# Subtracting the low parts of the feed-forward input on VectorE instead of GpSimd

## The chip, the cores and the metric

One core of a Trainium2 chip. The time is device microseconds of one launch, the median of three runs; the profile is that of one execution. The engines are TensorE (PE, with its weight loads as PEld), VectorE (DVE), ScalarE (ACT), GpSimd (POOL) and SyncE (SP), which issues the transfers.

## The reference

Block-causal attention over 64 heads (8 batches of 8 heads, 576 positions, 64 channels), then a low-rank mixing over positions and a feed-forward block with a residual.

```python
scores = scale * np.matmul(q, k.transpose(0, 1, 3, 2))
scores = np.where(mask, scores, -1000000000.0)
scores = scores - np.max(scores, axis=-1, keepdims=True)
attn = np.exp(scores)
attn = attn / (np.sum(attn, axis=-1, keepdims=True) + 1e-09)
attn_out = np.matmul(attn, v)
...
h = xt @ U @ V
u = x + h.transpose(0, 2, 1)
ch = np.maximum(u @ w_ch1, 0.0) @ w_ch2
return (u + ch).astype(np.float32)
```

## The kernel before, in words

Products are made more exact by splitting an operand into a high part (a cast to fp32r) and a low part (the operand less its high part), and adding three products: high by high, high by low, low by high.

Attention goes head by head: scores (L962 for the first 12 heads, L966 and L967 after them), row maxima on VectorE (L980, tile mx), exponentials on ScalarE (L991, p), reciprocal row sums on VectorE (L1007, L1008, rv), the rows multiplied by them on GpSimd (L1017, p), transposes on TensorE (L1050), from head 10 on a high and a low part of the transposed rows (ph on ScalarE L1027, pl on VectorE L1069), and the products with v (L1109, before that L1093). After every second head the mixing of two heads (`mix`) ends in the products of L1163; its small operand t3 has its low rows written by VectorE in L1154 (32x128, two inputs in SBUF). L1168 adds its result to attention's: that is u, 128 of the 512 channels.

The hidden layer has 2048 columns. Its first half is done by `ffn_chunk`, for 16 chunks of 288 positions. A chunk has four blocks k of 128 channels. For each, ScalarE casts u to the high part uh (L445) and GpSimd subtracts it to get the low part ul (L447). Eight column blocks f follow, each of 12 products (L465: w1h by uh, w1l by uh, w1h by ul), a ReLU on ScalarE (hh, L470) and its low part on VectorE (hl, L473); then the second layer's products (L488) and the sum with the input on VectorE (L494, ot). The first two chunks are done in two passes of four blocks f, so that there are 18 sets of four subtractions, 72 in all. The tiles uh and ul exist once, so a set waits until TensorE has read the last one's. The second half of the hidden layer (`block_products`, L659) follows when attention and the first half are done; its weights are loaded and combined by VectorE (L331 to L345, L548, L551) once attention has ended.

The order on all engines is set by the class `Plan`: each step is added with an engine, a cost in ns, a priority and its buffers, and `issue` plays the steps out in an event simulation, giving each free engine the ready step of the lowest priority value. Attention has priorities from 10 to 64000, the chunks' products 1e6 and more (they fill what attention leaves of TensorE), the chunks' other steps, the subtraction among them, -1. A step with `port=True`, and every step of GpSimd, is only given out while no other such step is running in the simulation. The instructions stand in the order so found, and each engine takes its own in that order.

```python
for x in later:
    heapq.heappush(q, x)
...
port = port or tasks[n][7]
end = now + tasks[n][1]
```

Of the kernel before, what the change touches and what calls it, by code (L numbers as in the profile page):

```python
# [26 lines left out]
T = 288  # L27
# [110 lines left out]
class Plan:  # L138
# [8 lines left out]
    def add(self, engine, ns, prio, fn, reads=(), writes=(), hold=(), after=0, port=False):  # L147

        n = len(self.tasks)
        deps = set()  # L150
        for b in reads:
            deps.update(b.writers)
            b.readers.append(n)
        for b in hold:
            deps.update(b.readers, b.writers)
        for b in writes:
            deps.update(b.readers, b.writers)
            b.writers, b.readers = [n], []
        deps.discard(n)
        slots = {b for b in (*reads, *writes) if b.pool is not None}  # L160
        for b in slots:
            b.users += 1
        self.tasks.append((engine, ns, prio, fn, deps, after, slots, port or engine == "POOL"))
# [76 lines left out]
def _act(n, sbuf=False):  # L240
    return (93 if sbuf else 52) + 0.833 * n


def _dve(n):
    return 69 + 1.042 * n


def _pe(*ns, m=()):

    m = [*m, *[P] * len(ns)][1 : len(ns)] + [P]  # L250
    return sum(max(0.85 * w, n * COL) for n, w in zip(ns, m))
# [3 lines left out]
def attention_then_mixer(  # L255
# [10 lines left out]
    nc = tc.nc  # L266
# [10 lines left out]
    def f32(ap):  # L277
        return ap.bitcast(F32)
# [29 lines left out]
    def take(r, name):  # L308
        n = used[name] = used.get(name, -1) + 1
        return r[n % len(r)]  # L310
# [120 lines left out]
    def ffn_chunk(c, w, wb, fr=range(FC), turn=0):  # L431

        b, o = c // CPB, (c % CPB) * T
        banks, done = banks_f if c < NCHUNK - 1 else Part(banks_f, banks_f), ffn_done[c]
        E, F = -1.0, 1e6 + (1300 + 300 * c if turn else 1000 * c)
        ur = ur_r[c % 2]
        for k in range(KC):
            if b > 0 or turn:
                add(
                    "SP", 630, E, lambda k=k: nc.sync.dma_start(out=ur[k].ap, in_=u_d[b][:, k, o : o + T]),  # L440
                    u_s[b][k].parts, [ur[k]], after=DL,
                )
        for k in range(KC):
            uh, ul = uh_r[k], ul_r[k]
            add("ACT", _act(T, True), E, lambda u=ur[k], h=uh: nc.scalar.copy(h.ap, u.ap), [ur[k]], [uh])  # L445
            add(
                "POOL", 780, E, lambda u=ur[k], h=uh, l=ul: nc.gpsimd.tensor_sub(l.ap, u.ap, f32(h.ap)),  # L447
                [ur[k], uh], [ul],
            )
            if turn:  # L450
                add(
                    "SP", 630, E, lambda k=k: nc.sync.dma_start(out=ur[k].ap, in_=o_d[b][:, k, o : o + T]),
                    [o_s[c][k]], [ur[k]], after=DL,
                )
        hs = {}
        for f in fr:
            ps = Buf(pool=banks)
            fs = slice(f * P, (f + 1) * P)
            ops = [(wn, k, m) for wn, m in (("w1h", uh_r), ("w1l", uh_r), ("w1h", ul_r)) for k in range(KC)]
            for g in range(0, len(ops), GM):  # L460

                def products(g=g, ps=ps, fs=fs, ops=ops):
                    for i in range(g, g + GM):
                        wn, k, m = ops[i]
                        nc.tensor.matmul(ps[:, :T], w()[wn][:, k, fs], m[k].ap, start=(i == 0), stop=(i == len(ops) - 1))  # L465

                sub = ops[g : g + GM]
                add("PE", _pe(*[T] * GM), F, products, [m[k] for _, k, m in sub] + [wb["w1"][f * P // CW][k] for _, k, _ in sub], [ps])
            th, tl = take(hh_r, "hh"), take(hl_r, "hl")
            add("ACT", _act(T), E, lambda ps=ps, th=th: nc.scalar.activation(th.ap, ps[:, :T], AF.Relu), [ps], [th])  # L470
            add(
                "DVE", _dve(T), E,
                lambda ps=ps, th=th, tl=tl: nc.vector.scalar_tensor_tensor(  # L473
                    out=tl.ap, in0=ps[:, :T], scalar=0.0, in1=f32(th.ap), op0=ALU.max, op1=ALU.subtract
                ),
                [ps, th], [tl],
            )
            hs[f] = (th, tl)
        for m in range(KC):
            ps = Buf(pool=banks)  # L480
            ms = slice(m * P, (m + 1) * P)
            ops = [(wn, f, x) for f in fr for wn, x in (("w2h", 0), ("w2l", 0), ("w2h", 1))]
            for g in range(0, len(ops), GM):

                def products(g=g, ps=ps, ms=ms, ops=ops):
                    for i in range(g, g + GM):
                        wn, f, x = ops[i]
                        nc.tensor.matmul(ps[:, :T], w()[wn][:, f, ms], hs[f][x].ap, start=(i == 0), stop=(i == len(ops) - 1))  # L488

                sub = ops[g : g + GM]  # L490
                add("PE", _pe(*[T] * GM), F, products, [hs[f][x] for _, f, x in sub] + [wb["w2"][f] for _, f, _ in sub], [ps])
            ot = take(ot_r, "ot")
            add(
                "DVE", _dve(T), E, lambda ps=ps, ot=ot, m=m: nc.vector.tensor_add(ot.ap, ps[:, :T], ur[m].ap),  # L494
                [ps, ur[m]], [ot],
            )
            done.writers.append(len(plan.tasks) - 1)
            add(
                "SP", 630, E, lambda ot=ot, m=m: nc.sync.dma_start(out=o_d[b][:, m, o : o + T], in_=ot.ap), [ot],
                [o_s[c][m]], after=DL,  # L500
            )
# [723 lines left out]
    for n in range(2):  # L1225
        for c in range(CPB):
            ffn_chunk(c, lambda: wa, wab, range(n * FH, (n + 1) * FH), n)
    for c in range(CPB, NCHUNK):
        ffn_chunk(c, lambda: wa, wab)
# [40 lines left out]
```

## Time and profile before

| | |
|---|---|
| median of 3 runs | 1183.15 us (1181.67 to 1183.31) |
| the profiled execution | 1182.37 us |
| its span, first to last instruction | 1180.6 us |
| busy: TensorE, weight loads | 1164.1 us (99%), 1131.4 us (96%) |
| busy: VectorE, ScalarE, GpSimd | 936.2 us (79%), 774.9 us (66%), 451.2 us (38%) |
| instructions of GpSimd, of VectorE | 582, 2009 |

Shares over the whole span are averages over three stages: attention with the first half as fill (to about 657 us), the rest of the first half (to about 820 us), and the second half. GpSimd works in the first two alone. Products of TensorE overlap, so that a product of 288 columns is shown with 0.29 us where one starts every 0.13 us.

### The profile page before, as it was taken

The page shows a single profiled execution, that of the slowest core. Times are in us where ns is not written, and L with a number is a line of the kernel's source. Part 1 is how long each engine was busy: PE and PEld are TensorE (multiplying, and loading weights), DVE is VectorE, ACT ScalarE, POOL GpSimd, SP SyncE. Part 2 cuts the span into 40 slices and gives each one's busy share as a digit, 9 for nine tenths or more (in the row PEclk, how much of TensorE's full clock was granted, in tenths as well). Part 3 has the DMA queues.
Part 4 walks back from the last instruction along what each step waited for, and adds up shares of the span by engine and source line. Part 5 has one row for each costly group of instructions (what it writes and reads, how often), then busy time and mean ns, then how long its engine had stood idle before and what let it go on. Part 6 is the DMA issues. An engine that isn't in the chain of part 4 may idle for free.

```text
span 1180.6 us, 25204 instructions
## 1 busy us (share of the span) xinstructions
PE 1164.1 (99%) x8988; PEld 1131.4 (96%) x8988; DVE 936.2 (79%) x2009; ACT 774.9 (66%) x1924; POOL 451.2 (38%) x582
## 2 busy tenths in 40 slices
PE   9989999999999999999999999999999999999998
PEld 7778999999999999999999999999999999999998
DVE  6898887877887877777877587327989889889887
ACT  7888888989888888898887342114544444444443
POOL 5556876676757666766674122110000000000000
PEclk9999999999999999999999999999999999999999
DMA  4445565433433433443331434211132132132121
GB/s 142 141 153 154 160 177 140 116 115 108 114 112 110 123 105 111 114 117 110 112 94 52 142 113 145 66 52 50 61 122 71 51 121 70 53 121 62 60 81 41
DMA packets 75884, 122.69 MB, mean 104 GB/s; under 512 B 8944, under 2 KB 52976, under 8 KB 75760
## 3 DMA queue, kind: packets, MB, share of 16 engines
q1 hardware_dynamic: 75760, 121.09, 34.8%
q8 instruction: 71, 1.16, 0.4%
q14 instruction: 53, 0.43, 0.1%
HBM read 76.23 MB, written 29.49 MB: 90 GB/s over the span
## 4 chain that ended last, share of the span: by engine, by line
PE 81%; DVE 8%; ACT 7%; issue 2%; DMA 1%; SPq 0%; POOL 0%; ACTq 0%; DVEq 0%; POOLq 0%
PE bb L659 30%; PE bf L465 11%; PE bf L488 10%; PE ba L1050 7%; PE ba L1109 6%; PE bg L488 4%; PE bg L465 4%; ACT p L991 3%; DVE mx L980 2%; PE ba L967 2%; PE ba L966 2%; PE ba L1134 1%; PE bw L966 1%; PE ba L1148 1%; DVE pl L1069 1%
## 5 line engine op out<-in xcount | busy, mean ns | idle before, releaser
L1017 POOL TENSOR_SCALAR p<-p,rv 128x192 f32<-128x192 f32 (+4 forms) x320 | 171.8, 551 | 156.8 <-DVE rv L1008 85.2
L659 PE MATMUL bb<-hh,w1l 128*128 128x288 f32 x704 | 170.1, 295 | 0.0
L659 PE MATMUL bb<-hh,w1h 128*128 128x288 f32 x704 | 169.4, 295 | 0.0
L1069 DVE TENSOR_TENSOR pl<-ba,ph 128x512 fp32r<-128x512 f32 x216 | 113.7, 550 | 17.9 <-ACT ph L1027 15.7
L991 ACT ACTIVATE p<-ba,mx 128x448 f32<-128x448 f32 (+2 forms) x248 | 114.8, 466 | 16.4 <-DVE mx L980 12.8
L1050 PE MATMUL ba<-ident,p 128*128 128x128 f32 x768 | 122.8, 275 | 2.7 <-POOL p L1017 1.5
L659 PE MATMUL bb<-hl,w1h 128*128 128x288 f32 x576 | 123.0, 295 | 0.1
L659 PEld LDWEIGHTS bb<-hh,w1l 128*128 128x128 f32 x704 | 122.9, 190 | 0.0
L659 PEld LDWEIGHTS bb<-hh,w1h 128*128 128x128 f32 x704 | 121.9, 188 | 0.0
L488 PE MATMUL bf<-hh,w2h 128*128 128x288 f32 x384 | 118.8, 309 | 0.9 <-DVE hl L473 0.9
L488 PE MATMUL bf<-hl,w2h 128*128 128x288 f32 x384 | 113.5, 295 | 0.0
L488 PE MATMUL bf<-hh,w2l 128*128 128x288 f32 x384 | 112.7, 294 | 0.0
L447 POOL TENSOR_TENSOR ul<-ur,uh 128x288 fp32r<-128x288 f32 x72 | 61.5, 880 | 127.2 <-PE bf L465 80.9
L613 ACT CAST hh<-hb 128x576 fp32r<-128x576 f32 x98 | 65.9, 672 | 60.6 <-PE bb L659 59.3
L1027 ACT CAST ph<-ba 128x512 fp32r<-128x512 f32 x216 | 98.8, 491 | 9.1 <-PE ba L1050 7.8
L980 DVE TENSOR_REDUCE mx<-ba 128x1 f32<-128x448 f32 (+3 forms) x248 | 95.1, 406 | 10.1 <-PE ba L967 7.5
L1050 PEld LDWEIGHTS ba<-ident,p 128*128 128x128 f32 x768 | 89.9, 141 | 8.3 <-POOL p L1017 3.4
L659 PEld LDWEIGHTS bb<-hl,w1h 128*128 128x128 f32 x576 | 91.9, 188 | 0.4 <-DVE hl L614 0.4
L1109 PE MATMUL ba<-ph,vs 128*128 128x256 f32 (+3 forms) x432 | 89.9, 262 | 0.0
L465 PE MATMUL bf<-uh,w1l 128*128 128x288 f32 x392 | 82.1, 305 | 0.0
L913 POOL TENSOR_TENSOR k<-raw,k 64x576 fp32r<-64x576 f32 x52 | 75.1, 1444 | 2.1 <-POOL p L1017 0.5
L912 POOL TENSOR_TENSOR q<-raw,q 64x576 fp32r<-64x576 f32 x52 | 74.0, 1422 | 4.5 <-issue 2.1
(173 smaller groups left out, 3357.7 us busy)
## 6 DMA issues: line engine op xcount, KB each, us to landing
raw<-in_qk_dram SPq DMA_DIRECT2D x63, 288.0 KB, 3.9
st<-in_w_dram SPq DMA_DIRECT2D x32, 512.0 KB, 3.7
o_d<-ot SPq DMA_DIRECT2D x72, 144.0 KB, 1.8
vr<-in_v_dram SPq DMA_DIRECT2D x32, 320.0 KB, 3.7
ur<-u_d SPq DMA_DIRECT2D x64, 144.0 KB, 2.4
whole<-o_d SPq DMA_DIRECT2D x32, 288.0 KB, 3.1
out_dram<-whole SPq DMA_DIRECT2D x31, 288.0 KB, 2.2
ur<-u_d SPq DMA_DIRECT2D x30, 288.0 KB, 3.3
```

Of the source, the lines that this page charges most:

```text
L465: nc.tensor.matmul(ps[:, :T], w()[wn][:, k, fs], m[k].ap, start=(i == 0), stop=(i == len(ops) - 1))
L488: nc.tensor.matmul(ps[:, :T], w()[wn][:, f, ms], hs[f][x].ap, start=(i == 0), stop=(i == len(ops) - 1))
L659: nc.tensor.matmul(bank[:, i, :T], x()[:, w(k)], p.ap[:, k, :], start=first and n == 0, stop=last and n == len(ops) - 1)
L912: add("POOL", 1380, pr, lambda: nc.gpsimd.tensor_sub(q1[top], raw[top, 0:S], f32(q2[top])), [raw, q2], [q1])
L913: add("POOL", 1380, pr, lambda: nc.gpsimd.tensor_sub(k2[top], raw[top, S : 2 * S], f32(k1[top])), [raw, k1], [k2])
L980: lambda i=i, at=at: nc.vector.tensor_reduce(out=mx[: P if i else 64, i : i + 1], in_=view(i, at), op=ALU.max, axis=AX.XY if wide else AX. ...
L991: nc.scalar.activation(out.rearrange("p (j k) -> p j k", j=2) if wide else out, view(i, at), AF.Exp, bias=mx[:rows, i : i + 1], accum_out= ...
L1017: lambda x=x, rows=rows, i=i: nc.gpsimd.tensor_scalar(out=x, in0=x, scalar1=rv[:rows, i : i + 1], scalar2=1.0, op0=ALU.mult, op1=ALU.mult),
L1027: add("ACT", _act(n), pr, lambda: nc.scalar.copy(out(), inp()), reads, writes)
L1050: nc.tensor.transpose(out=bank[:, a : a + P], in_=pt_r[i][h % PB[i]][:, j * P : (j + 1) * P], identity=perm.ap)
L1069: "DVE", _dve(m), pr, lambda: nc.vector.tensor_sub(pl[:, low], bank[:, :m], f32(ph[:, low])), [bank, bh], [bl]
L1109: nc.tensor.matmul(bank[0 : c.stop, a:n], vs[:, j, c], x[:, _at(g, j)], start=(i == 0), stop=(i == len(ops) - 1))
```

## The change

The 72 subtractions go from GpSimd to VectorE. Their cost for the planner goes from 780 ns to its formula for VectorE (369 ns at 288 columns), and they are marked as users of the shared port.

```diff
             add("ACT", _act(T, True), E, lambda u=ur[k], h=uh: nc.scalar.copy(h.ap, u.ap), [ur[k]], [uh])
             add(
-                "POOL", 780, E, lambda u=ur[k], h=uh, l=ul: nc.gpsimd.tensor_sub(l.ap, u.ap, f32(h.ap)),
-                [ur[k], uh], [ul],
+                "DVE", _dve(T), E, lambda u=ur[k], h=uh, l=ul: nc.vector.tensor_sub(l.ap, u.ap, f32(h.ap)),
+                [ur[k], uh], [ul], port=True,
             )
```

Because a cost and an engine are changed, the planner finds another order for all engines. Counted over the whole program, GpSimd has 508 instructions for 580 and VectorE 2081 for 2009; TensorE, ScalarE and SyncE have the same number as before in another order.

The first subtraction, on VectorE early in the program (ul, ur and uh as above, z and st the weights in work, mx row maxima, rv reciprocal row sums):

```order
 L980 TENSOR_REDUCE mx_164<-ba_97 128x1
 L980 TENSOR_REDUCE mx_164<-ba_97 64x1
+L447 TENSOR_TENSOR ul_110<-ur_104,uh_106 128x288
 L331 TENSOR_SCALAR z_103<-z_103 128x512
 L332 TENSOR_SCALAR z_103<-z_103 128x512
```

It now stands between a row maximum and a step of the weights. On GpSimd, at the same place of the program (w1l is a low part of weights, p attention's rows), the order of before has:

```order
L1017 TENSOR_SCALAR p_0_148<-p_0_148,rv_166 128x448
L361 TENSOR_TENSOR w1l_213<-z_102,w1h_212 128x512
L447 TENSOR_TENSOR ul_110<-ur_104,uh_106 128x288
L1017 TENSOR_SCALAR p_1_151<-p_1_151,rv_167 128x576
L1017 TENSOR_SCALAR p_0_147<-p_0_147,rv_166 128x320
```

There the rows of p behind it now follow directly on w1l. Later in attention the subtractions come in sets of four. One of them on VectorE in the order of the change (xl and xh are the mixing's operands):

```order
L980 TENSOR_REDUCE mx_165<-bw 128x1
L1139 TENSOR_TENSOR xl_177<-ba_96,xh_176 128x512
L447 TENSOR_TENSOR ul_110<-ur_105,uh_106 128x288
L473 SCALAR_TENSOR_TENSOR hl<-bf_91,hh 128x288
L447 TENSOR_TENSOR ul_111<-ur_105,uh_107 128x288
L447 TENSOR_TENSOR ul_112<-ur_105,uh_108 128x288
L447 TENSOR_TENSOR ul_113<-ur_105,uh_109 128x288
L1139 TENSOR_TENSOR xh_176<-ba_98,xh_176 64x128
```

The set stands around hl of the chunk ahead, which waits for the same products. Over the whole program 52 of VectorE's 72 subtractions stand ahead of its last attention operation (L1168) and 20 behind it; of GpSimd's, 48 stood ahead of its last row of p. On TensorE the last product of attention (L1163) now stands among the first products of a later chunk. Before it stood among the second layer's products:

```order
L488 MATMUL bf_90<-hh,w2l_215 128x288
L488 MATMUL bf_90<-hl,w2h_214 128x288
L1163 MATMUL ba_96<-v_183,t_0_178 128x288
L1163 MATMUL ba_95<-v_183,t_0_178 128x288
L488 MATMUL bf_91<-hh,w2h_214 128x288
```

and now:

```order
L465 MATMUL bf_91<-ul_112,w1h_212 128x288
L465 MATMUL bf_91<-ul_113,w1h_212 128x288
L1163 MATMUL ba_95<-v_183,t_0_178 128x288
L1163 MATMUL ba_96<-v_183,t_0_178 128x288
L465 MATMUL bf_90<-uh_106,w1h_212 128x288
```

Behind that place there were 1224 of the 3072 products of L465 and L488, and now there are 1128, so 96 more of them are ahead of it.

## Rows read from the trace of the kernel before

**Rows 1.** Busy time (share of the span) and instructions, from the profile's page.
```profile
PE 1164.1 (99%) x8988; PEld 1131.4 (96%) x8988; DVE 936.2 (79%) x2009; ACT 774.9 (66%) x1924; POOL 451.2 (38%) x582
```
**Rows 2.** Table by stage: stretch, its length, busy us and instructions, clock, DMA.
```profile
0.00:100.00 100.00, 91.13 (x529) 74.23 (x529) 82.74 (x214) 80.91 (x225) 57.09 (x85) 1.00 0.46 142
100.00:200.00 100.00, 97.94 (x783) 93.98 (x783) 86.34 (x213) 85.82 (x237) 74.77 (x90) 1.00 0.58 165
200.00:650.00 450.00, 447.77 (x3710) 436.43 (x3709) 353.48 (x955) 389.99 (x1101) 296.63 (x385) 1.00 0.38 107
650.00:810.00 160.00, 160.00 (x1212) 159.98 (x1211) 81.94 (x151) 47.81 (x103) 22.74 (x24) 1.00 0.31 97
810.00:1181.00 371.00, 367.25 (x2765) 366.77 (x2763) 331.67 (x479) 170.32 (x261) 0.00 (x0) 1.00 0.25 76
```
**Rows 3.** Waits of TensorE, 0 to 200 us: total us, times, longest.
```profile
PE ba L1050 <- POOL p L1017: 1.5, 2, 0.8
...
PE bf L488 <- DVE hl L473: 0.9, 1, 0.9
```
**Rows 4.** Waits of TensorE, 200 to 650 us: those for VectorE.
```profile
PE ba L1050 <- DVE xh L1139: 0.2, 1, 0.2
PE ba L1163 <- DVE ut L1168: 0.2, 1, 0.2
```
**Rows 5.** Costliest groups of the page: busy us, mean ns | idle before.
```profile
L447 POOL TENSOR_TENSOR ul<-ur,uh 128x288 fp32r<-128x288 f32 x72 | 61.5, 880 | 127.2 <-PE bf L465 80.9 <-PE bg L465 43.5 <-ACT uh L445 2.0
```
**Rows 6.** Waits of TensorE's weight loads over the whole span.
```profile
PEld ba L1050 <- POOL p L1017: 4.6, 11, 0.9
```
**Rows 7.** Lines L614 and L548 by source: shortest/median/longest ns, first and last start.
```profile
L614 DVE TENSOR_TENSOR hl<-ur,hh x46: 746/749/759, 819.3 to 1140.0; 128x576 fp32r<-128x576 f32 x46
...
L548 DVE TENSOR_TENSOR w1l<-whole,w1h x7: 1212/1217/1469, 664.3 to 706.9; 128x1024 fp32r<-128x1024 f32 x7
```
**Rows 8.** Groups of VectorE by line and form: busy us, mean ns | idle before.
```profile
L1168 DVE TENSOR_TENSOR ut<-ba,xt 128x288 f32<-128x288 f32 x56 | 23.9, 446 | 1.3 <-PE ba L1163 1.0
...
L1154 DVE TENSOR_TENSOR t<-tz,t 32x128 fp32r<-32x128 f32 x32 | 13.5, 422 | 2.6 <-ACT t L1153 1.8
```
**Rows 9.** Timeline of VectorE, 640 to 644 us: start us, length us.
```profile
642.44 0.81 DVE L1168 TENSOR_TENSOR ut<-ba,xt 128x288 f32<-128x288 f32 x2
```
**Rows 10.** Line L1154 by source: shortest/median/longest ns, first and last start.
```profile
L1154 DVE TENSOR_TENSOR t<-tz,t x32: 280/284/1526, 36.9 to 655.3; 32x128 fp32r<-32x128 f32 x32
```
**Rows 11.** Timeline of GpSimd, VectorE and TensorE between 322 and 327 us.
```profile
323.78 1.42 POOL L912 TENSOR_TENSOR q<-raw,q 64x576 fp32r<-64x576 f32 x1
...
323.82 1.53 DVE L1154 TENSOR_TENSOR t<-tz,t 32x128 fp32r<-32x128 f32 x1
...
326.62 0.29 PE L488 MATMUL bf<-hl,w2h 128*128 128x288 f32 x1
326.91 0.40 PE L1163 MATMUL ba<-v,t 96*128 96x288 f32 x1
```
**Rows 12.** Timeline of GpSimd, the subtractions: singles, then sets of four.
```profile
43.43 0.98 POOL L447 TENSOR_TENSOR ul<-ur,uh 128x288 fp32r<-128x288 f32 x1
...
113.63 3.37 POOL L447 TENSOR_TENSOR ul<-ur,uh 128x288 fp32r<-128x288 f32 x4
...
192.42 3.09 POOL L447 TENSOR_TENSOR ul<-ur,uh 128x288 fp32r<-128x288 f32 x4
...
541.69 3.12 POOL L447 TENSOR_TENSOR ul<-ur,uh 128x288 fp32r<-128x288 f32 x4 [2.85 <-PE bf L465]
```
**Rows 13.** Timeline of TensorE, 99 to 101 us: the first fill product.
```profile
99.95 0.77 PE L465 MATMUL bf<-uh,w1h 128*128 128x288 f32 x4
```
**Rows 14.** Timeline of VectorE at 706 us and of TensorE at 819 us.
```profile
706.92 1.47 DVE L548 TENSOR_TENSOR w1l<-whole,w1h 128x1024 fp32r<-128x1024 f32 x1
...
819.90 0.30 PE L659 MATMUL bb<-hh,w1h 128*128 128x288 f32 x1
```

## The prediction

> **What bounds the kernel now.** I read the busy shares first, then a table by stage, then who waits for whom in each stage. The profiled execution took 1182.37 us, its span is 1180.6 us, and TensorE is busy for 1164.1 us of that [rows 1], so the 16.5 us of visible idle time are about all that an edit of another engine can give back. The table says where these 16.5 us lie [rows 2]: 8.87 us in the first 100 us, before the feed-forward products can fill the gaps of attention; 2.06 us in the next 100; 2.23 us in the 450 us after that; nothing between 650 and 810 us; the rest is the tail. The granted clock is 1.00 in every stretch (the 2.4 GHz level), so it plays no part. VectorE is busy for 82.74, 86.34 and 353.48 us of the 100, 100 and 450 us of attention, near ScalarE and well above GpSimd. The waits of TensorE in the first 200 us are split over many lines; of the two engines of this change the largest are GpSimd's normalised rows (1.5 us) and VectorE's hl (0.9 us) [rows 3]. From 200 to 650 us only 0.4 us is put down to VectorE [rows 4]. The reader should see that the fill work makes TensorE deaf to most delays, and that this cover is absent before 100 us.
>
> **What is removed.** GpSimd loses 72 subtractions of 0.88 us on average, 61.5 us in all [rows 5]. GpSimd does not set the end. What the removal can give is what TensorE waits for GpSimd: 1.5 us at its products [rows 3], 4.6 us if every weight load held up by GpSimd is counted [rows 6]. Both ends stay in the range; I take the 1.5 us, because a load can wait while earlier products still run. In the order, the first subtraction vanishes ahead of a p row of GpSimd and appears on VectorE between a row maximum and a weight step.
>
> **What is added: the length of one.** No row shows this subtraction on VectorE. Its nearest relatives have two f32 inputs in SBUF and an fp32r output: 749 ns at 576 columns and 1217 ns at 1024 [rows 7], a slope of 1.04 ns a column, hence 749 - 288 x 1.04 = 449 ns at 288. An operation of the same width from PSUM takes 446 ns [rows 8], and two of them in a row 0.81 us [rows 9], so a second one in a row adds only 0.81 - 0.45 = 0.36 us. I take 0.37 us, the higher by the last digit, of VectorE's time for each: 72 x 0.37 = 26.6 us.
>
> **What is added: the wait for GpSimd.** VectorE has one operation with two SBUF inputs throughout attention, L1154 (32x128). Its mean is 422 ns [rows 8], its shortest 280 ns and its longest 1526 ns [rows 10]. At 323.82 us it begins just after a GpSimd subtraction that runs from 323.78 to 325.20 us, and ends at 325.35 [rows 11]. So such an operation can be held until GpSimd's ends, and the mean price is 422 - 280 = 142 ns. The planner marks L1154 and the moved subtraction alike (port=True), so I take 0.14 us for each of those that run while GpSimd is busy. The low end is 0. For the high end: GpSimd is busy 296.63 us of 450 with 385 instructions [rows 2]; without 32 subtractions it is about 60% busy with 0.77 us pieces, so a start at random waits 0.60 x 0.77 / 2 = 0.23 us.
>
> The Trainium skill, SBUF — State Buffer, section "SBUF: two separate sides", states this as a rule that speaks against the change: VectorE with two SBUF inputs and GpSimd take the shared port pair by an exclusive lock, and whichever comes second is blocked until the first one's instruction is over. The trace agrees, with 1.53 us in place of 0.28 at 323.82 us. By the rule with starts at random the waits sum to 52 x 0.23 = 12.0 us, by the row of L1154 to 52 x 0.14 = 7.3 us.
>
> **Where they lie.** By the new order 52 of the 72 stand ahead of the last attention operation of VectorE, 20 behind it. By the times of the old ones [rows 12], 4 come singly before the fill starts (43.43 us is the first of them; the first fill product is at 99.95 us [rows 13]), 16 in four sets between 100 and 200 us (113.63 the first, 192.42 the last), 32 in the rest of attention.
> The 20 behind attention cost nothing: VectorE is busy for 81.94 us of 160 there [rows 2]. What they could hold up is the second half's weights, whose last low part starts at 706.92 us and takes 1.47, against a first use at 819.90 us [rows 14]: a margin of 111 us. The new order leaves 1128 instead of 1224 fill products behind the last attention product. At 160 us for 1212 products [rows 2], 0.132 us each, that is 12.7 us less cover, and the 20 take 20 x 0.37 = 7.4 us: some 91 us of margin are left.
> The 4 before the fill have no cover, and stand in front of row maxima and weight steps that the first heads need: 4 x (0.37 + 0.14) = 2.0 us, taken in full.
> The 16 cost 16 x 0.51 = 8.2 us on VectorE, between 0 and 8.2 on TensorE. I pass them on in the ratio of TensorE's idle share there to that of the uncovered stretch, 2.06 / 8.87 = 0.23: 1.9 us.
> The 32 cost 16.3 us on VectorE. The same ratio is (2.23 / 4.5) / 8.87 = 0.056: 0.9 us. The case at 323.82 us supports a small share: VectorE lost 1.25 us, and the products of L1163 that depend on that operation lost little: the later one starts at 326.91, 0.29 us after the fill product ahead of it at 326.62, where 0.13 us is the normal distance [rows 11], so 0.16 us.
> One more wait moves: a subtraction waits until TensorE has read the old low part, and the set at 541.69 us stood 2.85 us for that on GpSimd, the longest such wait during attention [rows 12]. On VectorE, hl, row maxima and pl are queued behind it. I take nothing for it, since hl of the same chunk waits for the same products just beside it in the order; the high end is the 2.85 us, once.
>
> **Sum.** 2.0 + 1.9 + 0.9 - 1.5 = +3.3 us. Against the profiled execution that is 1185.7; the median of the runs shown is 0.78 us above it, so I forecast 1183.15 + 3.3 = 1186.4 us (+0.28%).
>
> **Rivals.**
> *All of it is hidden* (0.32). The planner knows the new cost and puts fill where attention comes late; TensorE stays full. For it: 2.23 us of idle in 450, and the harmless 1.25 us. Against it: the first 100 us have no fill. Time: 1183 us, within 2.4 us, which is the 0.2% that a measurement of this kernel can tell from no change.
> *GpSimd's relief decides: faster* (0.16). Sets of four hold GpSimd for 3.37 us [rows 12] in front of the normalisations that transposes wait for. If those come earlier, and VectorE's additions fall into the 17 and 14 us that it is idle in the first two stretches [rows 2], the sum is left with the relief alone: -1.5 us [rows 3] to -4.6 us [rows 6], so 1178.6 to 1181.7, say 1180. It decides if TensorE's idle time before 200 us falls from 10.9 to below 9 us. Against it: the new order finishes attention 96 fill products later, not earlier.
> *The waits for GpSimd decide: clearly slower* (0.15). If starts are as good as random and the product behind has no slack, each wait reaches TensorE: 52 x 0.23 = 12.0 us, about 1195 us. It decides once VectorE's subtractions average above some 0.7 us during attention and TensorE's idle time from 200 to 650 us goes above 8 us. Against it: the planner leaves VectorE's port operations until it believes GpSimd idle, and L1154's mean is only 0.14 us over. The Trainium skill's rule quoted above (SBUF — State Buffer, the same section) is what would make it so.
> That the change does not do what it says is excluded by the order: GpSimd loses 72 and VectorE gains 72 of the same shape.
>
> **Numbers.** My forecast has 0.37, with a range of its own from 1185.5 to 1190 us. Faster 0.16 and same 0.32 are the rivals above; slower is 0.37 + 0.15 = 0.52. The range runs from 1179.5 us, which leaves out the larger half of the relief, to 1195 us, which takes in the 16 at their full 8.2 us together with the 2.85 us, and ends at the price of the waits.
>
> **What would show it.** Right: L447 on VectorE at 0.45 us undisturbed and about 0.6 us on average; idle time of TensorE up by 1 to 4 us in the first 200 us and by under 2 us from 200 to 650; first product of L659 at about 823 us instead of 819.90; everything behind it unchanged in length. Wrong: the first product of the second half waiting for its weights; TensorE's idle time before 200 us falling; or waits for VectorE from 200 to 650 us of many microseconds.

## The result, and the profile after

The changed kernel takes 1186.44 us (median of 8 runs, 1184.86 to 1187.54) against 1182.53 us for the kernel before, measured beside it: a ratio of 1.0027, 95% interval 1.0015 to 1.0040. (Ratios here are formed from all the runs, and can differ by some 0.001 from the quotient of the medians, 1.0033 here.) The forecast was 1186.4 us. The profiled execution took 1185.76 us, its span 1184.0 us.

Busy shares of the changed kernel, from its page, against [rows 1]:

```profile
PE 1163.3 (98%) x8988; PEld 1132.5 (96%) x8988; DVE 961.3 (81%) x2081; ACT 773.7 (65%) x1924; POOL 393.0 (33%) x510
```

GpSimd has lost 58.2 us, VectorE has gained 25.1, TensorE does the same products. The table by stage (columns as in [rows 2]) says where the 3.4 us of span come from:

```profile
0.00:100.00 100.00, 89.17 (x506) 72.31 (x507) 79.84 (x214) 78.73 (x220) 51.10 (x79) 0.98 0.46 140
100.00:200.00 100.00, 97.44 (x775) 93.03 (x773) 90.92 (x223) 85.82 (x237) 65.02 (x73) 1.00 0.54 161
200.00:650.00 450.00, 446.00 (x3698) 437.13 (x3698) 363.31 (x970) 383.67 (x1086) 273.11 (x351) 1.00 0.38 108
650.00:810.00 160.00, 160.00 (x1227) 159.81 (x1227) 93.64 (x196) 52.55 (x119) 3.80 (x8) 1.00 0.31 99
```

TensorE's idle time is up by 1.96 us in the first 100 us, by 0.50 in the second, by 1.77 from 200 to 650, and by nothing behind. The second half's first and last products (timeline of TensorE):

```profile
823.33 0.30 PE L659 MATMUL bb<-hh,w1h 128*128 128x288 f32 x1
...
1180.39 0.43 PE L659 MATMUL bb<-hl,w1l 128*128 128x288 f32 x2
```

The first stood at 819.90 us [rows 14], so it is 3.43 us late; from there to the last product it is 357.06 us, and 357.05 before (its last product began at 1176.95). All of the loss lies ahead of the second half.

The subtraction on VectorE, grouped by form and then by source, against [rows 5]:

```profile
L447 DVE TENSOR_TENSOR ul<-ur,uh 128x288 fp32r<-128x288 f32 x72 | 36.6, 550 | 1.6 <-ACT uh L445 0.9 <-PE bg L465 0.7
...
L447 DVE TENSOR_TENSOR ul<-ur,uh x72: 427/450/1681, 43.4 to 786.5; 128x288 fp32r<-128x288 f32 x72
```

The median is 450 ns, the mean 550 and the longest 1681. The worst place is one set during attention, here from the timelines of VectorE, GpSimd and TensorE between 588 and 594 us:

```profile
589.34 4.07 DVE L447 TENSOR_TENSOR ul<-ur,uh 128x288 fp32r<-128x288 f32 x4
593.44 0.28 DVE L1139 TENSOR_TENSOR xh<-ba,xh 64x128 fp32r<-64x128 f32 x1
...
588.43 1.49 POOL L1017 TENSOR_SCALAR p<-p,rv 128x320 f32<-128x320 f32 x3 [5.32 <-ACT hh L470]
589.89 1.63 POOL L912 TENSOR_TENSOR q<-raw,q 64x576 fp32r<-64x576 f32 x1
591.48 1.61 POOL L913 TENSOR_TENSOR k<-raw,k 64x576 fp32r<-64x576 f32 x1
...
593.78 0.52 PE L1148 MATMUL ba<-xh,ust 128*64 128x128 f32 x5 [1.57 <-DVE xh L1139]
```

Four subtractions that need 4 x 0.37 = 1.5 us by the prediction take 4.07: the last two take 1.68 and 1.65 us, each ending 0.32 us behind a GpSimd operation that runs beside it; xh, next in VectorE's queue, comes late and TensorE stands still for 1.57 us. This is the cost that the prediction looked for. The largest waits of TensorE, however, lie elsewhere (whole span):

```profile
PE ba L1093 <- DVE pw L1025: 2.6, 1, 2.6
PE ba L1148 <- DVE xh L1139: 2.0, 3, 1.6
PE bw L962 <- ACT raw L902: 2.0, 2, 1.1
PE ba L1050 <- POOL p L1017: 1.2, 2, 0.9
```

The first one is new. Its place, on the timelines of VectorE, GpSimd and TensorE from 64 to 73 us:

```profile
65.01 1.83 DVE L895 CAST k<-raw 64x576 fp32r<-64x576 f32 x1
...
69.12 0.40 DVE L1025 COPY pw<-ba 128x256 f32<-128x256 f32 x1
...
65.25 1.27 POOL L361 TENSOR_TENSOR w2l<-z,w2h 128x512 fp32r<-128x512 f32 x1
...
69.58 3.40 PE L1093 MATMUL ba<-pw,vr 128*128 128x256 f32 x10 [2.56 <-DVE pw L1025]
```

No subtraction runs between 62 and 73 us. A cast of constants (L895), alone 0.45 us, takes 1.83 beside a GpSimd operation that ends at 66.52 us; the copy that TensorE needs is behind it in VectorE's queue. After 2.56 us of rest TensorE's products are slow. The table by single microseconds, columns as before:

```profile
69.00:70.00 1.00, 0.42 (x2) 0.39 (x3) 1.00 (x3) 0.04 (x1) 0.00 (x0) 1.00 0.00 0
70.00:71.00 1.00, 1.00 (x5) 0.80 (x4) 1.00 (x3) 0.00 (x0) 0.00 (x0) 0.56 0.00 0
71.00:72.00 1.00, 1.00 (x4) 0.82 (x3) 0.96 (x3) 0.00 (x0) 0.00 (x0) 0.50 0.00 0
72.00:73.00 1.00, 1.00 (x7) 1.00 (x6) 0.12 (x1) 0.00 (x0) 0.00 (x0) 0.50 0.00 0
73.00:74.00 1.00, 1.00 (x5) 0.72 (x5) 0.39 (x2) 0.53 (x2) 0.00 (x0) 0.73 0.80 209
```

The granted clock is at 0.50, the lower of its two levels (1.2 GHz), for some 3 us. So two theories stand against each other: **E**, the engine: VectorE's added time and its waits for GpSimd cost the microseconds; **O**, the order: the planner's new order costs them, whoever subtracts.

### The profile page after: what moved, and what is told of

Its sections match the earlier page's. It is cut to its first block, busy times and chain, and to the rows that moved or that the text cites. A ratio compares the mean times of both kernels' runs of the same rounds, so it can differ in the third digit from the quotient of the medians.

```text
span 1184.0 us, 25115 instructions
## 1 busy us (share of the span) xinstructions
PE 1163.3 (98%) x8988; PEld 1132.5 (96%) x8988; DVE 961.3 (81%) x2081; ACT 773.7 (65%) x1924; POOL 393.0 (33%) x510
## 4 chain that ended last, share of the span: by engine, by line
PE 81%; DVE 10%; ACT 6%; issue 2%; DMA 1%; SPq 0%; POOL 0%; DVEq 0%; ACTq 0%; POOLq 0%
PE bb L659 30%; PE bf L465 11%; PE bf L488 9%; PE ba L1050 7%; PE ba L1109 6%; PE bg L488 4%; PE bg L465 3%; ACT p L991 2%; PE ba L967 2%; PE ba L966 2%; DVE mx L980 2%; DVE ul L447 1%; PE ba L1093 1%; PE ba L1148 1%; DVE pl L1069 1%
## 5 line engine op out<-in xcount | busy, mean ns | idle before, releaser
L1017 POOL TENSOR_SCALAR p<-p,rv 128x192 f32<-128x192 f32 (+4 forms) x320 | 174.2, 559 | 203.6 <-DVE rv L1008 116.3
L991 ACT ACTIVATE p<-ba,mx 128x448 f32<-128x448 f32 (+3 forms) x248 | 114.8, 466 | 22.2 <-DVE mx L980 17.0
L488 PE MATMUL bf<-hh,w2h 128*128 128x288 f32 x384 | 119.7, 312 | 0.0
L488 PE MATMUL bf<-hl,w2h 128*128 128x288 f32 x384 | 113.5, 295 | 0.0
L488 PE MATMUL bf<-hh,w2l 128*128 128x288 f32 x384 | 112.8, 294 | 0.0
L465 PE MATMUL bf<-uh,w1l 128*128 128x288 f32 x412 | 85.6, 304 | 0.0
L465 PE MATMUL bf<-uh,w1h 128*128 128x288 f32 x412 | 74.8, 304 | 0.0
```

The costliest lines, as they stand in the source:

```text
L991: nc.scalar.activation(out.rearrange("p (j k) -> p j k", j=2) if wide else out, view(i, at), AF.Exp, bias=mx[:rows, i : i + 1], accum_out= ...
L1017: lambda x=x, rows=rows, i=i: nc.gpsimd.tensor_scalar(out=x, in0=x, scalar1=rv[:rows, i : i + 1], scalar2=1.0, op0=ALU.mult, op1=ALU.mult),
```

## The experiments

Order and engine can be taken apart, because the planner's record of a step (engine and cost) and the instruction that it issues are two arguments of one call. Each kernel was measured beside the kernel before on the same chip; ratios are against that. Its median lay between 1182 and 1183 us each time, so times are also compared across experiments.

**The old order, executed by VectorE, and the new order, executed by GpSimd.** TensorE's order is then exactly that of the kernel before, and exactly that of the change.

```diff
 # e1: order of before
-                "POOL", 780, E, lambda u=ur[k], h=uh, l=ul: nc.gpsimd.tensor_sub(l.ap, u.ap, f32(h.ap)),
+                "POOL", 780, E, lambda u=ur[k], h=uh, l=ul: nc.vector.tensor_sub(l.ap, u.ap, f32(h.ap)),
 # e2: order of the change
-                "DVE", _dve(T), E, lambda u=ur[k], h=uh, l=ul: nc.vector.tensor_sub(l.ap, u.ap, f32(h.ap)),
+                "DVE", _dve(T), E, lambda u=ur[k], h=uh, l=ul: nc.gpsimd.tensor_sub(l.ap, u.ap, f32(h.ap)),
```

> The planner still takes the 72 subtractions for GpSimd's (780 ns), so TensorE's order is that of before, but VectorE executes them. Theory E (VectorE's added time and its waits for GpSimd cost the 3 to 4 us): slower than before by at least as much as the change, 1185.5 to 1190 us, with TensorE's idle time up above all before 200 us. Theory O (the re-planned order of everything costs them, whoever subtracts): 1181 to 1184.5 us, within 0.2% of before.

> The order found for VectorE, the one of the change, but GpSimd executes the 72 subtractions. Theory E: the cost is gone, 1180 to 1184.5 us. Theory O: the cost stays, 1185 to 1188 us, and the wait of 2.56 us for the copy to pw near 69 us and the lower clock behind it are still there. If that wait goes although the order stays, it came from VectorE's added work.

Measured: e1 1192.49 us, ratio 1.0077 (1.0062 to 1.0092); e2 1183.74 us, ratio 1.0002 (0.9993 to 1.0011). E holds for the larger part. VectorE costs 1186.44 - 1183.74 = 2.7 us in the order that was planned for it, and about 10 in the order that was not, more than the 1190 us at most that I had given E. The order's own part cannot be told from zero by e2's ratio.

Since TensorE runs the same instructions in the same order in each pair, the same product can be looked up in both traces, and the difference of its times shows where time is lost. The mixing products L1163 of e1:

```profile
93.49 0.78 PE L1163 MATMUL ba<-v,t 96*128 96x288 f32 x2
...
139.77 0.38 PE L1163 MATMUL ba<-v,t 96*128 96x288 f32 x1
...
212.47 0.29 PE L1163 MATMUL ba<-v,t 96*128 96x288 f32 x1
...
666.74 0.43 PE L1163 MATMUL ba<-v,t 96*128 96x288 f32 x2
```

and the same four of the kernel before:

```profile
93.82 0.78 PE L1163 MATMUL ba<-v,t 96*128 96x288 f32 x2
...
138.22 0.40 PE L1163 MATMUL ba<-v,t 96*128 96x288 f32 x1
...
208.82 0.29 PE L1163 MATMUL ba<-v,t 96*128 96x288 f32 x1
...
657.11 0.43 PE L1163 MATMUL ba<-v,t 96*128 96x288 f32 x2
```

The lag is -0.33 us past the four single subtractions, +1.55, then +3.65 past the four sets, and +9.63 at the end. It grows at the sets and hardly between them. Without the planner's knowledge each set behind the singles costs about 0.9 us on average (10 us over 11 sets), the singles nothing. So 6.0 of the 9.6 us lie behind 209 us, and not above all before 200, as E had it.

For the changed kernel against e2 the same reading gives 2.1 us in all. Rows of L1163 in the changed kernel:

```profile
210.55 0.43 PE L1163 MATMUL ba<-v,t 96*128 96x288 f32 x2
...
573.40 0.38 PE L1163 MATMUL ba<-v,t 96*128 96x288 f32 x1
...
600.40 0.53 PE L1163 MATMUL ba<-v,t 96*128 96x288 f32 x2
...
673.28 0.43 PE L1163 MATMUL ba<-v,t 96*128 96x288 f32 x2
```

and in e2:

```profile
209.14 0.43 PE L1163 MATMUL ba<-v,t 96*128 96x288 f32 x2
...
572.73 0.38 PE L1163 MATMUL ba<-v,t 96*128 96x288 f32 x1
...
598.60 0.43 PE L1163 MATMUL ba<-v,t 96*128 96x288 f32 x2
...
671.20 0.43 PE L1163 MATMUL ba<-v,t 96*128 96x288 f32 x2
```

VectorE is 1.41 us behind at 210 us, gains back 0.74 until 573, loses 1.13 at the set of 589 us and 0.28 just behind it, and ends 2.08 behind. The lag is net, what VectorE adds less what GpSimd's relief gives back: in e2 TensorE waits 4.3 us for GpSimd's rows p, in the changed kernel 1.2 (waits of TensorE in e2):

```profile
PE ba L1050 <- POOL p L1017: 4.3, 5, 1.2
```

The wait of 2.56 us and the low clock are in e2 as well (2.58 us), so it is not the subtractions on VectorE that make them. The second half begins in e2 at

```profile
821.25 0.30 PE L659 MATMUL bb<-hh,w1h 128*128 128x288 f32 x1
```

1.35 us later than before, with the wait and the clock in it.

**The first five sets alone, and the others alone.**

```diff
-                "POOL", 780, E, lambda u=ur[k], h=uh, l=ul: nc.gpsimd.tensor_sub(l.ap, u.ap, f32(h.ap)),
-                [ur[k], uh], [ul],
+                *(
+                    ("DVE", _dve(T), E, lambda u=ur[k], h=uh, l=ul: nc.vector.tensor_sub(l.ap, u.ap, f32(h.ap)))
+                    if c < 3 else        # e3; e4: c >= 3
+                    ("POOL", 780, E, lambda u=ur[k], h=uh, l=ul: nc.gpsimd.tensor_sub(l.ap, u.ap, f32(h.ap)))
+                ),
+                [ur[k], uh], [ul], port=True,
```

> Only the five sets of chunks 0, 1 (both passes) and 2 go to VectorE, planned as such; the other 13 stay on GpSimd. The order is that of the change up to the first set of chunk 3, near 235 us. Theory E as sized in the prediction: 2.0 + 1.9 - 1.5 = +2.4 us, about 1185 to 1186 us, with TensorE's idle time before 200 us at 13 to 13.5 us as in the change. Theory O gives the same for this stretch, and afterwards what the new order makes of it.

> The complement: the five first sets stay on GpSimd, the 13 later ones go to VectorE. The order is that of before up to about 235 us. Theory E: TensorE's idle time before 200 us as before (10.9 us), from 200 to 650 us up by 0.9 to 1.8 us, so 1183.5 to 1185 us. Theory O: anything within 1181 to 1187, not tied to VectorE's waits for GpSimd.

Measured: e3 1186.95 us, ratio 1.0028 (1.0016 to 1.0040); e4 1180.05 us, ratio 0.9977 (0.9967 to 0.9987). With five sets moved the whole loss is there, more than E's 1185 to 1186 us; but e3's order has the wait for pw (2.6 us) and the low clock near 70 us too, so it does not price the five sets alone. With the 13 others moved the kernel is faster than before, which E did not allow, and faster than the 1181 us at which O's range began. The groups of VectorE by form, of e3 and then of e4 (line numbers moved by the edit):

```profile
L448 DVE TENSOR_TENSOR ul<-ur,uh 128x288 fp32r<-128x288 f32 x20 | 11.8, 626 | 0.3 <-ACT uh L445 0.3
```

```profile
L448 DVE TENSOR_TENSOR ul<-ur,uh 128x288 fp32r<-128x288 f32 x52 | 21.1, 451 | 0.7 <-PE bf L469 0.4 <-PE bg L469 0.3
```

The 20 early ones wait 0.18 us each on average (626 - 450); the 52 of e4 wait for nothing. So waits for GpSimd are not a tax on every such operation: under e4's order the subtractions did not meet GpSimd, in the early part of the other order they did.

**Is e4 faster because GpSimd is relieved, or by its order?** e5 has e4's order, and GpSimd executes all 72.

```diff
-                    ("DVE", _dve(T), E, lambda u=ur[k], h=uh, l=ul: nc.vector.tensor_sub(l.ap, u.ap, f32(h.ap)))
+                    ("DVE", _dve(T), E, lambda u=ur[k], h=uh, l=ul: nc.gpsimd.tensor_sub(l.ap, u.ap, f32(h.ap)))
                     if c >= 3 else
```

> The order of the run with the 13 later sets on VectorE, but GpSimd executes all 72. If that run gained because GpSimd was relieved (theory R): the gain goes, 1182 to 1184 us. If it gained because its order is a better one, whoever subtracts (theory O): 1178 to 1181 us, and no slower than with VectorE.

Measured: 1179.02 us, ratio 0.9972 (0.9962 to 0.9982). It is the order. By the medians GpSimd runs it 1 us faster than VectorE, within the intervals; the products of L1163 (L1167 in these two kernels) show where. e5 is 0.38 us ahead of e4 at 209 us, where the two have run identical instructions, and 1.46 at the end of attention, here in e4 and then in e5:

```profile
659.14 0.43 PE L1167 MATMUL ba<-v,t 96*128 96x288 f32 x2
```

```profile
657.68 0.42 PE L1167 MATMUL ba<-v,t 96*128 96x288 f32 x2
```

That is 1.1 us for the 32 subtractions between, although these do not wait for GpSimd. e5 is also the fastest version of the study, 3.8 us below the kernel before. What makes its order better is not settled.

**How far does a new order alone move the kernel?** e7 changes one number, so that no work moves.

```diff
-                "POOL", 780, E, lambda u=ur[k], h=uh, l=ul: nc.gpsimd.tensor_sub(l.ap, u.ap, f32(h.ap)),
+                "POOL", 806, E, lambda u=ur[k], h=uh, l=ul: nc.gpsimd.tensor_sub(l.ap, u.ap, f32(h.ap)),
```

> The kernel before with one number changed: the planner takes 806 ns (the median of the trace) for the subtraction on GpSimd in place of 780. No work moves; only the order is found anew. Theory O (order alone moves this kernel by microseconds): more than 2.4 us away from before, to either side, within 1178 to 1190. Theory E: within 0.2% of before, 1180.2 to 1184.9.

Measured: 1182.71 us, ratio 1.0000 (0.9991 to 1.0010). Of the three new orders run wholly on GpSimd, two (e2, e7) cannot be told from the old one and one (e5) is 0.28% better. In these three a new order moved the kernel by at most 4 us.

**The cast near 65 us.** e6 keeps the order of the change, and ScalarE executes the casts of L895.

```diff
-                    "DVE", _dve(S) / 2, pr, lambda x=x, o=o: nc.vector.tensor_copy(x[64:P, :], raw[64:P, o : o + S]),
+                    "DVE", _dve(S) / 2, pr, lambda x=x, o=o: nc.scalar.copy(x[64:P, :], raw[64:P, o : o + S]),
```

> The order of the change, all 72 subtractions on VectorE, but the four casts of constants for heads 10 and 11 (L895) are executed by ScalarE, in the place where they stood for VectorE. If the wait of 2.56 us near 69 us and the low clock behind it come from the cast that stood behind GpSimd (1.83 us for 0.45): the wait falls below 1.2 us, the clock stays at 1.00, and the time falls by 2 to 4 us, to 1182.5 to 1184.5. If the wait comes from VectorE's load as such: 1185.5 to 1187.5, and the clock still falls.

Measured: 1184.47 us, ratio 1.0011 (1.0002 to 1.0019), 2.0 us faster than the change. The wait shrank as expected (waits of TensorE in e6):

```profile
PE ba L1093 <- DVE pw L1025: 0.6, 1, 0.6
```

In the profiled execution the clock did not recover: from 65 to 70 us it is 0.85, from 70 to 75 us 0.81. That half of the expectation failed there; TensorE is still idle for 1.62 of the 5 us from 65 to 70, 0.82 of it for a copy (xt) that ScalarE does after the cast it was given, and the clock falls at the same place. Over all executions it did recover in part: the mean granted clock is 1.000 in 5 of 11, and in none of the 8 of the change.

**Behind attention only.** e8 is e4 with `c >= 11`.

> Only the sets of chunks 11 to 15, which run behind attention where GpSimd has nothing else, go to VectorE (20 subtractions). The prediction put nothing on these: 1181.5 to 1183.7 us, as before; TensorE busy for all of 650 to 810 us. A cost here (over 1185 us) would say that the second half's weights came late.

Measured: 1182.22 us, ratio 1.0007 (0.9997 to 1.0017): nothing that can be told from zero.

**The early ones by themselves.** The order of the change, with GpSimd executing the four singles (e9) or the first twenty (e10).

```diff
-                lambda u=ur[k], h=uh, l=ul: nc.vector.tensor_sub(l.ap, u.ap, f32(h.ap)),
+                lambda u=ur[k], h=uh, l=ul: (nc.gpsimd if c == 0 and not turn else nc.vector).tensor_sub(l.ap, u.ap, f32(h.ap)),
 # e10: nc.gpsimd if c < 3
```

> The order of the change, but GpSimd executes the four single subtractions that stand before the fill work. The prediction took 2.0 us in full for them: by that, 2.0 us faster than the change, about 1184.5 us. By the comparison of the two executions with the order of the change (VectorE against GpSimd) they cost at most 0.5 us: then 1186 us, within 0.1% of the change.

> The order of the change, GpSimd executing the first twenty subtractions (the four singles and the four sets up to 200 us) and VectorE the 52 others. By the prediction's terms 2.0 + 1.9 us are gone: about 1182.5 us. By the comparison of executions 1.1 us are gone: about 1185.2 us. The wait of 2.56 us near 69 us should be there in both runs, because it comes from the order.

Measured: e9 1185.39 us, ratio 1.0025 (1.0015 to 1.0035); e10 1185.19 us, ratio 1.0024 (1.0012 to 1.0036). The change itself stands at 1.0027. Both are nearer to the smaller figures. By the products of L1163, e9 is 1.0 us ahead of the change at 96 us, so the singles cost between 0 (e1) and 1 us; executions of identical instructions differ there by up to 0.6 us (e4 and e5), so a closer value is not to be had.

The profiled execution of e10 tells something else. Its wait near 69 us is there, but not the low clock:

```profile
69.26 2.06 PE L1093 MATMUL ba<-pw,vr 128*128 128x256 f32 x10 [2.58 <-DVE pw L1025]
```

and by single microseconds:

```profile
70.00:71.00 1.00, 1.00 (x7) 0.91 (x6) 0.97 (x3) 0.00 (x0) 0.00 (x0) 1.00 0.00 0
71.00:72.00 1.00, 1.00 (x8) 0.84 (x8) 0.89 (x3) 0.53 (x2) 0.00 (x0) 1.00 0.00 0
72.00:73.00 1.00, 1.00 (x10) 1.00 (x9) 0.89 (x2) 0.50 (x2) 0.00 (x0) 1.00 0.24 53
```

The ten products take 2.06 us here and 3.40 in the changed kernel. Up to this place e10 and e2 run the same instructions on the same engines; from there e2 is 1.5 us behind e10. The first product of L1163 behind it, in e10 and then in e2:

```profile
77.65 0.51 PE L1163 MATMUL ba<-v,t 96*128 96x288 f32 x2
```

```profile
79.19 0.51 PE L1163 MATMUL ba<-v,t 96*128 96x288 f32 x2
```

The distance was 0.14 us at 59 us and stays at 1.5 up to 234. That is what the low clock costs.

In e9 the wait near 69 us is 2.3 us, but the cast L895 takes only 0.46 there. In its place a step of the weights is held, one with one input in SBUF too, which takes 0.42 us when nothing holds it:

```profile
65.89 2.15 DVE L331 TENSOR_SCALAR z<-z 128x512 f32<-128x512 f32 x1
```

Up to there e9 runs the same instructions as e2 and e10, where the cast is held. So the order makes the place, and which operation is held there changes from one execution to the next. The set of 589 us is uneven in the same way. In e10 it is longer than the 4.07 us of the changed kernel (timeline of VectorE):

```profile
586.38 4.88 DVE L447 TENSOR_TENSOR ul<-ur,uh 128x288 fp32r<-128x288 f32 x4
```

Its first subtraction is held while two GpSimd operations run one behind the other (3.11 us, in e9 3.12), and the longest wait of TensorE for xh is 2.9 us in both, where it was 1.57.

## Why the prediction was right, and which of its steps were not

The time, the sign and the place of the loss came out, and so did the signs that I had named: 550 ns on average, TensorE's idle time up by 2.46 us before 200 us and by 1.77 up to 650, the second half's first product at 823.33 us. The make-up of the sum did not in all parts, and that the time was met is in part luck. The sum priced the move of the work at +3.3 us. By the traces that move costs 2.08 us (against e2), and another 1.35 us, which the sum does not have, come with the new order.

- **Length of one: right.** 449 ns forecast, median 450.
- **Waits for GpSimd: right in sum.** 52 x 0.14 = 7.3 us forecast; 72 x (0.550 - 0.450) = 7.2 us measured. L1154 as a stand-in served, though it is the only such operation only behind 175 us (until then the steps of the weights in L337 and L345 have two inputs in SBUF as well). But the waits are uneven: one set lost 2.5 us, and in e4 52 of them lost nothing. Not in the sum is that VectorE's other operations are held less once GpSimd has fewer: L1154's mean is 398 ns in the changed kernel and 504 in e2. The rule of the Trainium skill (SBUF — State Buffer, section "SBUF: two separate sides") is borne out at 589 us, where subtractions of 0.45 us take 1.68 and 1.65 beside GpSimd's operations; what it leaves open, how often such operations meet, is set by the order.
- **The 4 before the fill, 2.0 us "taken in full": the failed step.** No fill covers that stretch, but it does not follow that VectorE's delay ends last there. e1 shows nothing for them, e9 at most 1.0 us, and the changed kernel is 0.8 us behind e2 at 96 us.
- **The 16, 1.9 us: not to be told apart.** The lag of the changed kernel against e2 grows by 1.41 us up to 210 us, with the singles and GpSimd's relief in it; forecast for the three was 2.0 + 1.9 - 1.5 = 2.4, so the whole stretch was priced 1.0 us too high.
- **The 32, 0.9 us: right in size, by luck.** 0.67 us against e2 from 210 us to the end of attention, and 1.1 us in e4 against e5. But it is not one small share of every set: a single set costs 1.4 us, 0.74 is won back ahead of it, and with the same 32 on VectorE e10 loses 1.5 us against e2 over this stretch and e9 3.1, with a second stretch of low clock in it. The ratio of idle shares was a guess that happened to serve.
- **GpSimd's relief, -1.5 us: there, but not where the row of before put it.** The early waits for p fell from 1.5 us [rows 3] to 0.9, and to 0.9 in e2 too, so that much is the order. In that order GpSimd's 72 subtractions would cost TensorE 4.3 us of waits for p, 2.0 of them between 100 and 210 us; on VectorE it is 1.2 in all, and none there. Other waits took the place of part of it.
- **Missing: the new order itself.** The sum counted what moves, not what the re-planned order does to work that stays. By trace that is +1.35 us (e2), and in it the wait of 2.56 us for a cast and a copy that have nothing to do with the subtraction, and the low clock of 1.5 us, partly made good elsewhere. The prediction left the clock out because the trace of before showed 1.00 throughout; here it failed. Nearly all of the 1.35 us goes with the clock: e2's three executions with a mean granted clock of 1.000 took 1182.1 to 1182.2 us, and the 17 such of the kernel before, measured beside them, have a median of 1182.3. The term made up for what I had taken too much.
- **Nothing behind attention: right.** e8, and TensorE busy for all of 650 to 810 us.
- **The wait for TensorE's reads: right to leave out.** VectorE's subtractions waited 0.7 us for it in all, none of it during attention.

Of the rivals, "hidden" fell because singles and sets do reach TensorE before 210 us and at 589. "Waits decide" fell: the idle time from 200 to 650 us is 4.00 us, not 8. "Relief" fell on its own sign: TensorE's idle time before 200 us should have gone below 9 us, and is 13.4.

## What to carry to other kernels

Where a planner sets the order, an edit is two edits, of the work and of the order; give the planner one engine and issue on another, and each can be measured alone. With one engine's instructions in the same order, subtracting the times of the same instruction in two traces shows step by step where the time goes, and is finer than the medians, as long as both ran at the same clock: here the same instructions differed by up to 0.6 us between two executions, and by 1.5 us where one had the low clock. An uncovered stretch is not a stretch in which every delay counts: look for who ends last there before pricing a delay in full.

## What the runs showed of the hardware

I had not expected the clock. After 2.6 us without products TensorE ran at the lower level (granted 0.50) for about 3 us in the changed kernel and in e2, and in e10's profiled execution, after the same wait of 2.58 us, it did not. The same goes for 2.9 us without products near 590 us: behind them the clock fell to 0.50 in e9 and stayed at 1.00 in e10. So the same stretch of program costs 1.5 us more or not from one execution to another, and a profile shows one of the two. Medians hold a mixture: the mean granted clock was below 1.000 in 26 of the 80 executions of the kernel before, which went with about 2 us (medians of 1184.2 to 1184.7 us against 1181.9 to 1182.3), and in all 8 of the changed kernel. What decides which it will be, no run here shows. Nor had I expected casts with one input in SBUF, such as L895, to be held as long as subtractions with two: 1.83 us for 0.45, beside a GpSimd operation, and in e9 a step of the weights (L331) 2.15 us for 0.42.
